# A linear-attention block with an MLP: two float32 products between the halves, done as hi and lo one-pass products

## The chip, the cores and the metric

The kernel runs on one core of a Trainium2 chip, in one launch. The metric is the device time in microseconds. Before the change three runs took 881.53, 881.9 and 882.74 us, so the median is 881.9 us. The engines that matter are TensorE (PE; its weight loads are shown as PEld), VectorE (DVE), ScalarE (ACT), GpSimd (POOL) and SyncE (SP), which issues all the DMAs here.

## What is computed

The input is one sequence of 2048 tokens of width 448. Two layers run, each a linear attention block (half A) and a GELU MLP (half B), both behind a layer norm and with a residual.

```python
def _A_ref(x, wqkv, wo):                       # H = 16 heads, Dh = 28
    qkv = (x @ wqkv) ...                       # q, k, v per head
    phi = lambda t: jnp.where(t > 0, t + 1, jnp.exp(t)) + 1e-6
    pq, pk = phi(q), phi(k)
    kv = jnp.einsum("bhsd,bhse->bhde", pk, v)
    z = jnp.einsum("bhsd->bhd", pk)            # sum of pk over the tokens
    num = jnp.einsum("bhqd,bhde->bhqe", pq, kv)
    den = jnp.einsum("bhqd,bhd->bhq", pq, z)[..., None] + 1e-6
    return (num / den) ... @ wo

x = x + _A_ref(_layernorm(x), A_wqkv, A_wo)
x = x + _B_ref(_layernorm(x), B_w1, B_b1, B_w2, B_b2)   # gelu(x @ w1 + b1) @ w2 + b2
x = x + _A_ref(_layernorm(x), A_wqkv, A_wo)
x = x + _B_ref(_layernorm(x), B_w1, B_b1, B_w2, B_b2)
```

## The kernel before

Tokens are worked in 16 tiles of 128. Nearly every matrix product is done with float32r operands, which TensorE takes in one pass. To keep the precision, an operand is split into a hi part (the value rounded to float32r, a copy) and a lo part (what is left, a subtraction), and a product is the sum of hi times hi, hi times lo and lo times hi, three one-pass products into the same PSUM bank. A few products are done in native float32 instead: the transposes, kvp, and the two that this change is about, zp and mp.

A layer has three parts. In **phase 1** (phase1, L542) each tile is normalised, k is projected (psk), phi is applied, the result pk is split into kh and kl, and the product G of x (xnh, xnl) with pk is accumulated in four PSUM banks over all tiles (stage_g, L473, four groups c = 0 to 3). VectorE also adds pk into za (L444). Most of the tiles' q projections (psq) are done here too and their phi is stored to DRAM as pq; the last seven are kept back to fill TensorE later. In the first layer the MLP's weights are split in the background (ScalarE copies w2h, GpSimd subtracts w2l, L352 and L353).

Then comes the **transition**, whose order is written out by hand in the string ORDER (L491). Each token calls one small function, and every engine runs its instructions in the order in which they are called:

- Q: a q projection of a kept-back tile. Qp (fill_qphi, L462): its phi, three ScalarE operations and one GpSimd addition (eq, L470), and the store to DRAM.
- G: the last tile's part of the product G.
- z (trans_z, L610): zp = ones times za, so that each of 128 partitions holds the sum of z over all tokens; ScalarE copies it to zb; VectorE makes dc from it.
- gt (L620): ScalarE copies the four banks of G to SBUF. kv (L627): kvp, the product of wv with gt, all heads at once. mask (L634): VectorE keeps the blocks on the diagonal of each head, in kvm.
- m0 to m3 (trans_m, L640): mp = kvm times wo, one group g of 112 rows each. ms (trans_ms, L645): its split into Mh (ScalarE) and Ml (VectorE).
- ld0 to ld3: loads of pq and x of the four tiles of block 0. qz (q_z, L681): GpSimd multiplies pq with zb, giving pz. qs (q_scale, L685): VectorE sums pz per head (dn, L689), adds dc (L690), takes the reciprocal (L692) and scales pq (L694). tq (L697): TensorE transposes the scaled pq into a PSUM bank. qq (q_split, L706): its split into qh (ScalarE) and ql (VectorE).
- o0 to o3 (o_mm, L716): pq times M, twelve one-pass products a tile. la, lb, T, x: residual, layer norm, transpose and split for the MLP.

zp, kvp and the tq share two PSUM banks (tag "m"), taken in turn, so a tq waits until the bank of the one before last has been read, which is when that tile's ql is done. mp and the output products share four (tag "acc").

The third part is the **MLP** (mlp1 L780, mlp2 L799): four blocks of four tiles, 14 steps each, with the next block's attention output worked behind it.

SBUF buffers are shared by tags: "E" and "F" (two each) hold kh and kl, "xn" (two) the background weights in the first layer and later the normalised rows, "H" (nine) the rows of x, "W6" kvm.

Of the kernel before, what the change touches and what calls it, by code (L numbers as in the profile page):

```python
# [10 lines left out]
F32R = mybir.dt.float32r  # L11
AF = mybir.ActivationFunctionType
OP = mybir.AluOpType
# [9 lines left out]
def linear_attn_mlp_kernel(  # L23
# [12 lines left out]
    pe, act, dve, pool, sp = nc.tensor, nc.scalar, nc.vector, nc.gpsimd, nc.sync  # L36
# [25 lines left out]
    def bank(tag, bufs, name):  # L62
        return psum.tile([128, 512], F32, name=name, tag=tag, bufs=bufs)
# [3 lines left out]
    def t448(tag, bufs, name, dt=F32):  # L67
        bufs = NH if tag == "H" else bufs
        return work.tile([128, D], dt, name=name, tag=tag, bufs=bufs)

    def t512(tag, bufs, name, dt=F32):
        return work.tile([128, 512], dt, name=name, tag=tag, bufs=bufs)

    def f(ap):
        return ap.bitcast(F32)
# [4 lines left out]
    def load_x(l, t):  # L80
        xt[l, t] = t448("H", 8, f"x{l}_{t}")
        sp.dma_start(xt[l, t], x_d[l][t * 128:(t + 1) * 128, :])
# [67 lines left out]

    ones = consts.tile([128, 128], F32, name="ones")
    dve.memset(ones, 1.0)
    warm = bank("m", 2, "warm")

    def warm_up(n):
# [295 lines left out]
    def stage_q(l, t, cs=range(4)):  # L451
        qs_[l, t] = proj("q", ("a", l, t // 4), t % 4, qs_.get((l, t)), cs)
        if 3 in cs:
            qo.append((l, t, qs_.pop((l, t))))

    def stage_qphi():
        while qo:
            l, t, o = qo.pop(0)
            e = phi(o, "eq")
            sp.dma_start(pq_d[l][t * 128:(t + 1) * 128, :], e)  # L460

    def fill_qphi():  # L462

        l, t, o = qo.pop(0)
        e = t512("e", 3, "eq")[:, :D]
        p = t512("E", 2, "ep")[:, :D]
        act.activation(e, o, AF.Relu, scale=-1.0)
        act.activation(p, o, AF.Relu)
        act.activation(e, e, AF.Exp, scale=-1.0)
        pool.tensor_tensor(e, p, e, op=OP.add)  # L470
        sp.dma_start(pq_d[l][t * 128:(t + 1) * 128, :], e)

    def stage_g(l, t, acc):  # L473
        h, lo = split.pop((l, t))
        kh, kl = ks.pop((l, t))
        first, last = t == 0, t == NT - 1
        for c in range(3):
            s = slice(c * 128, (c + 1) * 128)
            pe.matmul(acc[c], h[:, s], kh, start=first, stop=False)  # L479
            pe.matmul(acc[c], h[:, s], kl, start=False, stop=False)  # L480
            pe.matmul(acc[c], lo[:, s], kh, start=False, stop=last)  # L481
        pe.matmul(acc[3], h[:, TL:], kh, start=first, stop=False)
        pe.matmul(acc[3], h[:, TL:], kl, start=False, stop=last)

# [2 lines left out]


    ORDER = (  # L491
# [4 lines left out]
    )  # L496
# [110 lines left out]
            sp.dma_start(s, wo[h * 2 * G:(h + 1) * 2 * G, :].rearrange("(g p) n -> p g n", p=G))  # L607
            tr.wo += [s[:, 0], s[:, 1]]

    def trans_z(tr, za):  # L610
        zp = bank("m", 2, "zp")[:, :D]
        pe.matmul(zp, ones, za, start=True, stop=True)
        tr.zb = consts.tile([128, D], F32, name="zb", tag="za")
        act.activation(tr.zb, zp, AF.Identity, bias=zc)

        tr.dc = consts.tile([128, H], F32, name="dc", tag="dc")
        dve.tensor_reduce(tr.dc, tr.zb.rearrange("p (h d) -> p h d", d=DH), axis=mybir.AxisListType.X, op=OP.add)
        dve.tensor_scalar(tr.dc, tr.dc, 1e-6, 1e-6, op0=OP.mult, op1=OP.add)

    def trans_gt(tr, acc):  # L620
        tr.gt = []
        for c in range(4):
            s = t512("A" if c < 2 else "B", 2, "gt")[:, :D]
            act.copy(s, acc[c])
            tr.gt.append(s)
# [8 lines left out]
    def trans_mask(tr):  # L634
# [2 lines left out]
                          tr.kvp.rearrange("p (g d) -> p g d", g=NG),  # L637
                          mask[:, None, :].to_broadcast([G, NG, G]), op=OP.mult)

    def trans_m(tr, g):  # L640
        mp = bank("acc", 4, "mp")[:G, :D]
        pe.matmul(mp, tr.kvm[:, g * G:(g + 1) * G], tr.wo[g], start=True, stop=True)
        tr.mp[g] = mp

    def trans_ms(tr, g):  # L645
        if g == 0:
            tr.Mh, tr.Ml = [], []
        if g % 2 == 0:
            for n in ("Mh", "Ml"):
                s = work.tile([128, 1024], F32R, name=n, tag="S", bufs=5)  # L650
                getattr(tr, n).extend(s[:G, i * D:(i + 1) * D] for i in range(2))
        act.copy(tr.Mh[g], tr.mp[g])
        dve.tensor_sub(tr.Ml[g], tr.mp[g], f(tr.Mh[g]))

# [21 lines left out]
    def load_pq(l, b, j):  # L676
        t = b * 4 + j
        pqt[l, t] = t448(f"W{j}", 1, f"pq{l}_{t}")
        sp.dma_start(pqt[l, t], pq_d[l][t * 128:(t + 1) * 128, :])
# [36 lines left out]
    def o_mm(l, b, j, tr):  # L716
        qh, ql = qs.pop((l, b, j))
        o = ops[l, b, j] = bank("acc", 4, "op")[:, :D]
        for g in range(NG):
            s = slice(g * 128, (g + 1) * 128)  # L720
            pe.matmul(o, qh[:, s], tr.Mh[g], start=(g == 0), stop=False)
            pe.matmul(o, qh[:, s], tr.Ml[g], start=False, stop=False)
            pe.matmul(o, ql[:, s], tr.Mh[g], start=False, stop=(g == NG - 1))

    def oc_mm(l, b, j, tr):

# [175 lines left out]
    warm_up(2)  # L902

    for l in range(LAYERS):
        tr = SimpleNamespace(mp={})
        za, acc = phase1(l, tr)
        if l == 0:
            background(0)
        fill = list(range(DEFER, NT))

        def pre(j):
            for k in range(4):
                load_pq(l, 1, k)
            if l == 0:
                background(2)

        tok_ = SimpleNamespace(
            Q=lambda j: stage_q(l, fill.pop(0)), Qp=lambda j: fill_qphi(), Qv=lambda j: stage_qphi(), G=lambda j: stage_g(l, NT - 1, acc),
            ld=lambda j: (load_pq(l, 0, j), load_x(l, j)), z=lambda j: trans_z(tr, za), gt=lambda j: trans_gt(tr, acc),
            kv=lambda j: trans_kv(tr), mask=lambda j: trans_mask(tr), m=lambda j: trans_m(tr, j),  # L920
            ms=lambda j: trans_ms(tr, j), qz=lambda j: q_z(l, 0, j, tr), qs=lambda j: q_scale(l, 0, j, tr),
            tq=lambda j: q_transpose(l, 0, j), qq=lambda j: q_split(l, 0, j), o=lambda j: o_mm(l, 0, j, tr),
            la=lambda j: o_ln(l, 0, j), lb=lambda j: o_n(l, 0, j), T=lambda j: m_transpose(l, 0, j),
            x=lambda j: m_split(l, 0, j), pre=pre)
        for tok in ORDER.split():
            name, j = tok.rstrip("0123456789"), int("0" + tok.lstrip("abcdefghijklmnopqrstuvwxyzQTG"))
            getattr(tok_, name)(j)
        assert not fill and not qo
        table(AF.Gelu_apprx_tanh)
        q_z(l, 1, 0, tr)  # L930
        mlp1(l, 0, 0)
        trans_chunks(tr)
        for b in range(NB):
            acc = [bank("acc", 4, f"y{j}")[:, :D] for j in range(4)]
            nxt = b + 1 < NB
            if not nxt and l + 1 < LAYERS:
                st_k = stage_square(wqkv[:, D:2 * D])
                st_q = stage_square(wqkv[:, :D])
                load_to(l + 1, PRE - 1)
            for i in range(NF):  # L940
                if i + 1 < NF:
                    mlp1(l, b, i + 1)
                elif nxt:
                    mlp1(l, b + 1, 0)
                if l == 0 and b == 0 and i:
                    background(1, 1)
                if i == NF - 2 and not nxt and l + 1 < LAYERS:
                    table(AF.Exp)
                if 9 <= i < 13:
                    add_bias(l, b, i - 9)  # L950
                if nxt:
                    behind(l, b, i, tr)
                elif l + 1 < LAYERS:
                    if i == 2:
                        split_kq("k", st_k)
                    if i == 5:
                        split_kq("q", st_q)
                    if i in (3, 4, 6, 7, 8):
                        t = (3, 4, 6, 7, 8).index(i)
                        stage_a(l + 1, t)  # L960
                        stage_n(l + 1, t)
                        stage_t(l + 1, t)
                        if t % 2:
                            stage_sp(l + 1, t)
                    if 9 <= i < 13:
                        stage_x(l + 1, i - 9)
                mlp2(l, b, i, acc)
# [28 lines left out]
```

## Time and profile before

| | us |
|---|---|
| median of three runs | 881.9 |
| profiled execution, its own time | 881.78 |
| its span, from the first to the last instruction | 880.1 |
| TensorE busy in the span | 871.8 |
| transition, first layer (from zp to the MLP's first product) | 106.7 to 141.0 |
| transition, second layer | 538.5 to 572.8 |
| TensorE idle in each transition | 0.36 |

The profile is one execution. A busy share is the part of the span in which an engine had an instruction running. The timeline gives each instruction's start and length, in us from the span's start. The chain of waits follows what ended last back to the start. TensorE's one-pass products are pipelined: of 448 columns, one is shown with 0.37 us, but the next starts about 0.20 us after it, so their cost is read from start to start. A native float32 product is shown as two instructions (x2 for zp, x8 for the four mp). TensorE's granted clock was 1.00 in all of the transition.

In the transitions of the second layer VectorE was busy 24.8 of the 31.6 us from 538.5 to 570.1, ScalarE 13.8, and GpSimd 10.0.

### The profile page before, as it was taken

To read this page: it belongs to the slowest core of one execution; us is meant where nothing else is said; L and a number is where in the kernel's file an instruction comes from. 1 tells how busy PE (TensorE), PEld (TensorE's weight loads), DVE (VectorE), ACT (ScalarE), POOL (GpSimd) and SP (SyncE) were. 2 spreads that over 40 slices of the span, in tenths; PEclk is the share of its full clock that TensorE was granted. 3 is DMA by queue.
4 is the path that set the end of the run, shared out by engine and by line. 5 is a ranking of instruction groups with operands and counts; after the bars stand their busy time and mean duration, and the time that the engine had idled before them with its cause. 6 is when DMAs were issued, how large, how long until landed. Compare 5 with 4: busy or idle time off the path is not lost.

```text
span 880.1 us, 11693 instructions
## 1 busy us (share of the span) xinstructions
PE 871.8 (99%) x4190; PEld 773.4 (88%) x4190; DVE 485.6 (55%) x947; ACT 344.8 (39%) x609; POOL 221.1 (25%) x252
## 2 busy tenths in 40 slices
PE   8999999999999999999999999999999999999998
PEld 6999988888888888888899999888888888888887
DVE  6878585658455543226467866755574473432112
ACT  6576645324223322333355664442233133223221
POOL 5466633335012102011222333220220140140000
PEclk9999999999999999999999999999999999999999
DMA  5477715624413402051146443243332323111001
GB/s 156 148 213 223 218 53 159 199 78 140 132 59 104 156 0 96 1 178 48 48 136 196 153 144 95 63 152 101 104 114 91 112 75 131 49 49 40 3 1 42
DMA packets 62762, 93.71 MB, mean 106 GB/s; under 512 B 8816, under 2 KB 57968, under 8 KB 62704
## 3 DMA queue, kind: packets, MB, share of 16 engines
q1 hardware_dynamic: 62704, 92.97, 33.7%
q8 instruction: 33, 0.54, 0.3%
q14 instruction: 25, 0.20, 0.1%
HBM read 55.65 MB, written 34.08 MB: 102 GB/s over the span
## 4 chain that ended last, share of the span: by engine, by line
PE 96%; DVE 1%; POOL 1%; DMA 1%; ACT 1%; issue 0%; SPq 0%; POOLq 0%; ACTq 0%; DVEq 0%
PE y L806 10%; PE y L805 10%; PE y L804 10%; PE hp L787 9%; PE hp L786 9%; PE hp L788 9%; PE hp L789 3%; PE hp L790 3%; PE G L480 2%; PE G L481 2%; PE G L479 2%; PE psk L306 2%; PE psk L308 2%; PE psk L307 2%; PE psq L306 2%; PE psq L307 2%
## 5 line engine op out<-in xcount | busy, mean ns | idle before, releaser
L796 DVE TENSOR_TENSOR gl<-g,gh 128x512 fp32r<-128x512 f32 x112 | 82.7, 738 | 299.7 <-ACT gh L795 299.7
L792 ACT ACTIVATE g<-hp,b1s 128x512 f32<-128x512 f32 x112 | 77.0, 688 | 406.4 <-PE hp L790 406.4
L806 PE MATMUL y<-w2h,gl 128*128 128x448 f32 x448 | 163.9, 366 | 0.0
L805 PE MATMUL y<-w2l,gh 128*128 128x448 f32 x448 | 163.8, 366 | 0.0
L804 PE MATMUL y<-w2h,gh 128*128 128x448 f32 x448 | 163.8, 366 | 0.0
L787 PE MATMUL hp<-XH,w1l 128*128 128x512 f32 x336 | 131.7, 392 | 0.0
L786 PE MATMUL hp<-XH,w1h 128*128 128x512 f32 x336 | 131.4, 391 | 0.0
L788 PE MATMUL hp<-XL,w1h 128*128 128x512 f32 x336 | 131.2, 391 | 0.0
L203 POOL TENSOR_TENSOR brs<-bve,mhalf 128x1 f32<-128x1 f32 x64 | 38.9, 607 | 272.5 <-DVE bve L201 265.4
L804 PEld LDWEIGHTS y<-w2h,gh 128*128 128x128 f32 x448 | 84.2, 188 | 8.8
L805 PEld LDWEIGHTS y<-w2l,gh 128*128 128x128 f32 x448 | 84.3, 188 | 8.3
L806 PEld LDWEIGHTS y<-w2h,gl 128*128 128x128 f32 x448 | 84.3, 188 | 6.5
L788 PEld LDWEIGHTS hp<-XL,w1h 128*128 128x128 f32 x336 | 63.1, 188 | 13.6
L787 PEld LDWEIGHTS hp<-XH,w1l 128*128 128x128 f32 x336 | 63.2, 188 | 11.1
L786 PEld LDWEIGHTS hp<-XH,w1h 128*128 128x128 f32 x336 | 63.3, 188 | 10.9
L795 ACT CAST gh<-g 128x512 fp32r<-128x512 f32 x112 | 69.7, 622 | 3.6
L416 POOL TENSOR_TENSOR xnl<-x,xnh 128x384 fp32r<-128x384 f32 x32 | 35.7, 1117 | 84.4 <-ACT xnh L415 50.0
L683 POOL TENSOR_TENSOR pz<-pq,zb 128x448 f32<-128x448 f32 x32 | 36.6, 1148 | 79.7 <-DVE dn L689 65.3
L296 DVE TENSOR_TENSOR XL<-sp,XH 128x512 fp32r<-128x512 f32 x50 | 42.7, 861 | 5.3 <-ACT XH L295 5.3
L790 PE MATMUL hp<-XL,w1x 128*128 128x512 f32 x112 | 43.6, 389 | 0.0
L789 PE MATMUL hp<-XH,w1x 128*128 128x512 f32 x112 | 43.6, 389 | 0.0
L752 POOL TENSOR_TENSOR x<-x,b2b 128x448 f32<-128x448 f32 x32 | 41.9, 1332 | 0.0
(145 smaller groups left out, 1565.6 us busy)
## 6 DMA issues: line engine op xcount, KB each, us to landing
x<-in_A_x_dram SPq DMA_DIRECT2D x32, 224.0 KB, 3.7
pq_d<-eq SPq DMA_DIRECT2D x32, 224.0 KB, 2.9
pq<-pq_d SPq DMA_DIRECT2D x32, 224.0 KB, 3.2
x<-x_d SPq DMA_DIRECT2D x32, 224.0 KB, 3.6
sq_a<-sq SPq DMA_DIRECT2D x13, 512.0 KB, 2.9
sp<-sq_a SPq DMA_DIRECT2D x52, 128.0 KB, 3.0
sq_q<-sq SPq DMA_DIRECT2D x12, 512.0 KB, 2.6
sp<-sq_q SPq DMA_DIRECT2D x48, 128.0 KB, 3.1
```

The lines of the kernel that those rows point to most:

```text
L296: dve.tensor_sub(lo.rearrange("p (c i n) -> p c i n", c=4, n=32), x, f(h))
L786: pe.matmul(o, w1h[:, c, s], x.moving(x.hi, c), start=(c == 0), stop=False)
L787: pe.matmul(o, w1l[:, c, s], x.moving(x.hi, c), start=False, stop=False)
L788: pe.matmul(o, w1h[:, c, s], x.moving(x.lo, c), start=False, stop=False)
L789: pe.matmul(o, w1x[:, s], x.moving(x.hi, 3), start=False, stop=False)
L790: pe.matmul(o, w1x[:, s], x.moving(x.lo, 3), start=False, stop=True)
L792: act.activation(g, hp, AF.Gelu_apprx_tanh, bias=b1s[:, i:i + 1])
L795: act.copy(gh, g)
L796: dve.tensor_sub(gl, g, f(gh))
L804: pe.matmul(acc[j], gh[:, s], w2h[:, i], start=first, stop=False)
L805: pe.matmul(acc[j], gh[:, s], w2l[:, i], start=False, stop=False)
L806: pe.matmul(acc[j], gl[:, s], w2h[:, i], start=False, stop=last)
```

## The change

zp becomes two one-pass products, of ones with zh and with zl, the hi and lo parts of za; the ones get a float32r copy. mp becomes three for each group: kvh with woh, kvh with wol, kvl with woh. The splits are new work: zh, the four woh and kvh are copies on ScalarE, zl and kvl subtractions on VectorE, and the four wol subtractions on GpSimd. They take buffers from the tags E, F, xn and H. In ORDER the new tokens zs, kvs, wh and wl place them; the last tile's G is divided, its group c = 0 stands ahead of z and the others behind it; and the groups of m, ms and o_mm go in the order 2, 3, 0, 1.

```diff
+    ones_r = consts.tile([128, 128], F32R, name="ones_r")
+    dve.tensor_copy(ones_r, ones)
...
-    def stage_g(l, t, acc):
+    def stage_g(l, t, acc, cs=range(4)):
...
     ORDER = (
-        "Q ld1 z ld0 ld2 qz0 qz1 G gt qs1 Q Qp kv qs0 tq1 Q mask qz2 tq0 qs2 ld3 "
-        "m0 qq1 Qp m1 qz3 ms0 qq0 m2 ms1 m3 ms2 tq2 ms3 qs3 o0 la0 qq2 o1 tq3 lb0 la1 qq3 Qp pre "
+        "Q ld1 zs G0 z ld0 ld2 qz0 qz1 G1 wh2 wh3 gt qs1 wl2 wl3 Q Qp kv qs0 tq1 wh0 wh1 Q mask kvs qz2 wl0 wl1 tq0 qs2 ld3 "
+        "m2 qq1 Qp m3 qz3 ms2 qq0 m0 ms3 m1 ms0 tq2 ms1 qs3 o0 la0 qq2 o1 tq3 lb0 la1 qq3 Qp pre "
...
-    def trans_z(tr, za):
+    def trans_zs(tr, za):
+        tr.zh = t512("F", 2, "zh", F32R)[:, :D]
+        tr.zl = t512("E", 2, "zl", F32R)[:, :D]
+        act.copy(tr.zh, za)
+        dve.tensor_sub(tr.zl, za, f(tr.zh))
+
+    def trans_z(tr):
         zp = bank("m", 2, "zp")[:, :D]
-        pe.matmul(zp, ones, za, start=True, stop=True)
+        pe.matmul(zp, ones_r, tr.zh, start=True, stop=False)
+        pe.matmul(zp, ones_r, tr.zl, start=False, stop=True)
...
+    def trans_kvs(tr):
+        tr.kvh = t512("E", 2, "kvh", F32R)[:G, :D]
+        tr.kvl = t448("H", 8, "kvl", F32R)[:G]
+        act.copy(tr.kvh, tr.kvm)
+        dve.tensor_sub(tr.kvl, tr.kvm, f(tr.kvh))
+
+    def trans_wh(tr, g):
+        tr.woh[g] = t512("F" if g < 2 else "xn", 2, "woh", F32R)[:G, :D]
+        act.copy(tr.woh[g], tr.wo[g])
+
+    def trans_wl(tr, g):
+        tr.wol[g] = t448("H", 8, "wol", F32R)[:G]
+        pool.tensor_tensor(tr.wol[g], tr.wo[g], f(tr.woh[g]), op=OP.subtract)
+
     def trans_m(tr, g):
         mp = bank("acc", 4, "mp")[:G, :D]
-        pe.matmul(mp, tr.kvm[:, g * G:(g + 1) * G], tr.wo[g], start=True, stop=True)
+        s = slice(g * G, (g + 1) * G)
+        pe.matmul(mp, tr.kvh[:, s], tr.woh[g], start=True, stop=False)
+        pe.matmul(mp, tr.kvh[:, s], tr.wol[g], start=False, stop=False)
+        pe.matmul(mp, tr.kvl[:, s], tr.woh[g], start=False, stop=True)
...
-        for g in range(NG):
+        for g in (2, 3, 0, 1):
```

More of the change, by code (lines that the diff above doesn't have):

```diff
@@ L471, in fill_qphi @@
         sp.dma_start(pq_d[l][t * 128:(t + 1) * 128, :], e)
-    def stage_g(l, t, acc):
-        h, lo = split.pop((l, t))
-        kh, kl = ks.pop((l, t))
+    def stage_g(l, t, acc, cs=range(4)):
+        h, lo = split[l, t]
+        kh, kl = ks[l, t]
         first, last = t == 0, t == NT - 1
-        for c in range(3):
+        for c in cs:
+            if c == 3:
+                pe.matmul(acc[3], h[:, TL:], kh, start=first, stop=False)
+                pe.matmul(acc[3], h[:, TL:], kl, start=False, stop=last)
+                continue
             s = slice(c * 128, (c + 1) * 128)
@@ L481, in stage_g @@
             pe.matmul(acc[c], lo[:, s], kh, start=False, stop=last)
-        pe.matmul(acc[3], h[:, TL:], kh, start=first, stop=False)
-        pe.matmul(acc[3], h[:, TL:], kl, start=False, stop=last)
     ORDER = (
[2 rows of a table removed]
[2 rows of a table added]
         "o2 T0 lb1 la2 o3 x0 T1 Q lb2 la3 x1 T2 Q x2 lb3 Qp "
@@ L638, in trans_mask @@
                           mask[:, None, :].to_broadcast([G, NG, G]), op=OP.mult)
+    def trans_kvs(tr):
[9 more added lines that the diff above has]
+        pool.tensor_tensor(tr.wol[g], tr.wo[g], f(tr.woh[g]), op=OP.subtract)
     def trans_m(tr, g):
         mp = bank("acc", 4, "mp")[:G, :D]
-        pe.matmul(mp, tr.kvm[:, g * G:(g + 1) * G], tr.wo[g], start=True, stop=True)
+        s = slice(g * G, (g + 1) * G)
+        pe.matmul(mp, tr.kvh[:, s], tr.woh[g], start=True, stop=False)
+        pe.matmul(mp, tr.kvh[:, s], tr.wol[g], start=False, stop=False)
+        pe.matmul(mp, tr.kvl[:, s], tr.woh[g], start=False, stop=True)
         tr.mp[g] = mp
     def trans_ms(tr, g):
-        if g == 0:
-            tr.Mh, tr.Ml = [], []
         if g % 2 == 0:
-            for n in ("Mh", "Ml"):
-                s = work.tile([128, 1024], F32R, name=n, tag="S", bufs=5)
-                getattr(tr, n).extend(s[:G, i * D:(i + 1) * D] for i in range(2))
+            for m in (tr.Mh, tr.Ml):
+                s = work.tile([128, 1024], F32R, name="M", tag="S", bufs=5)
+                m[g], m[g + 1] = (s[:G, i * D:(i + 1) * D] for i in range(2))
         act.copy(tr.Mh[g], tr.mp[g])
@@ L718, in o_mm @@
         o = ops[l, b, j] = bank("acc", 4, "op")[:, :D]
-        for g in range(NG):
+        for g in (2, 3, 0, 1):
             s = slice(g * 128, (g + 1) * 128)
-            pe.matmul(o, qh[:, s], tr.Mh[g], start=(g == 0), stop=False)
+            pe.matmul(o, qh[:, s], tr.Mh[g], start=(g == 2), stop=False)
             pe.matmul(o, qh[:, s], tr.Ml[g], start=False, stop=False)
-            pe.matmul(o, ql[:, s], tr.Mh[g], start=False, stop=(g == NG - 1))
+            pe.matmul(o, ql[:, s], tr.Mh[g], start=False, stop=(g == 1))
     def oc_mm(l, b, j, tr):
@@ L904, in linear_attn_mlp_kernel @@
     for l in range(LAYERS):
-        tr = SimpleNamespace(mp={})
+        tr = SimpleNamespace(mp={}, Mh={}, Ml={}, woh={}, wol={})
         za, acc = phase1(l, tr)
@@ L917, in linear_attn_mlp_kernel @@
         tok_ = SimpleNamespace(
-            Q=lambda j: stage_q(l, fill.pop(0)), Qp=lambda j: fill_qphi(), Qv=lambda j: stage_qphi(), G=lambda j: stage_g(l, NT - 1, acc),
-            ld=lambda j: (load_pq(l, 0, j), load_x(l, j)), z=lambda j: trans_z(tr, za), gt=lambda j: trans_gt(tr, acc),
+            Q=lambda j: stage_q(l, fill.pop(0)), Qp=lambda j: fill_qphi(), Qv=lambda j: stage_qphi(),
+            G=lambda j: stage_g(l, NT - 1, acc, range(1, 4) if j else (0,)), zs=lambda j: trans_zs(tr, za),
+            kvs=lambda j: trans_kvs(tr), wh=lambda j: trans_wh(tr, j), wl=lambda j: trans_wl(tr, j),
+            ld=lambda j: (load_pq(l, 0, j), load_x(l, j)), z=lambda j: trans_z(tr), gt=lambda j: trans_gt(tr, acc),
             kv=lambda j: trans_kv(tr), mask=lambda j: trans_mask(tr), m=lambda j: trans_m(tr, j),
```

## The prediction

> **What bounds the kernel now.** I read the page first: its busy shares and the shares of the chain that ended last.
>
> ```profile
> PE 871.8 (99%) x4190; PEld 773.4 (88%) x4190; DVE 485.6 (55%) x947; ACT 344.8 (39%) x609; POOL 221.1 (25%) x252
> PE 96%; DVE 1%; POOL 1%; DMA 1%; ACT 1%; issue 0%; SPq 0%; POOLq 0%; ACTq 0%; DVEq 0%
> ```
>
> TensorE sets the time. Whatever shortens its own work is gained whole, and every wait put into its queue is lost whole. So I read the chain of waits in order of time (start us, us, what), here the middle part of the second layer.
>
> ```profile
> 538.67 0.75 PE zp L612 x2
> 543.87 3.14 PE kvp L632 x32
> 547.01 0.44 PE tq L701 x4
> 550.12 3.01 PE mp L642 x8
> 553.13 0.44 PE tq L701 x4
> ...
> 570.46 0.47 PE psq L306
> ```
>
> The two products that the change touches cost 0.75 us (zp) and 3.01 us (four mp), and from 538.5 to 570.1 TensorE never stands. The other engines have slack there, but how much depends on whether two of them can work at once. The timeline of VectorE (start, us, what), early in the MLP:
>
> ```profile
> 148.89 0.17 DVE L690 TENSOR_TENSOR dn<-dn,dc 128x16 f32<-128x16 f32 x1
> 149.38 1.18 DVE L694 SCALAR_TENSOR_TENSOR pq<-pq,rd 128x448 f32<-128x448 f32 x1
> ...
> 153.78 0.48 DVE L690 TENSOR_TENSOR dn<-dn,dc 128x16 f32<-128x16 f32 x1
> 154.58 1.23 DVE L694 SCALAR_TENSOR_TENSOR pq<-pq,rd 128x448 f32<-128x448 f32 x1
> ```
>
> and of GpSimd in the same stretch:
>
> ```profile
> 148.93 1.15 POOL L683 TENSOR_TENSOR pz<-pq,zb 128x448 f32<-128x448 f32 x1 [5.67 <-DMA wq<-Ml]
> 153.03 1.19 POOL L353 TENSOR_TENSOR w2l<-stg,w2h 128x448 fp32r<-128x448 f32 x1 [2.95 <-DMA wq<-Mh]
> 154.19 1.15 POOL L683 TENSOR_TENSOR pz<-pq,zb 128x448 f32<-128x448 f32 x1
> ```
>
> The same L690 takes 0.17 or 0.48 us and L694 0.62 (below) or 1.18 and 1.23. The long ones start inside a GpSimd instruction and end just after it: pz ends at 150.08, L694 at 150.56. A VectorE operation with both operands in SBUF waits for a running GpSimd operation; it gets in between two of them (L690 of 153.78 ends at 154.26, between w2l and pz). A blocked 0.62 us operation ends 0.48 us after the GpSimd one. Operations that read PSUM (kl L440, Ml L653) keep 0.62 us whatever GpSimd does. The Trainium skill, page "SBUF — State Buffer", section "Who interferes with whom", states this as an exclusive lock: two SBUF inputs on VectorE against a GpSimd instruction that reads SBUF, the first to start holds it for its whole length. By that rule the sum is the 886.5 us below, without it the 880.0 us of the first rival; the rows above agree with it.
>
> **What it removes on TensorE.** One-pass products of 448 columns start every 0.2035 us (eleven of psq: 536.28 to 538.51). zp: two of them, 0.41 for 0.75, gain 0.34. mp: 12 x 0.2035 = 2.44 for 3.01, gain 0.57. Together 0.91 a layer, 1.8 us in two. The Trainium skill, "TensorE: Matmul & The Clock Gate", section "Back-to-back issue gap", gives N/2.4 + 2.5 ns, an estimate of 0.189 us; by it the 14 products would save 0.2 us more a layer and the sum would be 886.1; the rows decide for 0.2035.
>
> **What it adds.** Per layer on ScalarE six copies (zh, four woh, kvh), SBUF to SBUF, 0.56 us each and 0.46 to the next (w2h L352, xnh L415); on VectorE zl and kvl, both operands in SBUF, 448 wide: between 0.62 (L694) and 0.67 (XL L296, 512 wide), taken 0.62; on GpSimd four wol, 1.13 to 1.20 by w2l L353, taken 1.15 with 1.11 to the next. The one copy into ones_r lies ahead of the warm-up where VectorE then waits 2.4 us for the first x; at most 0.3 us if that cover were gone. No DMA is added. On SP's queue the store of the first eq waits for GpSimd and the loads of pq3 and x3 stand behind it: eq ends 0.7 us later (below), pq3 lands near 546.4 + 3.2 = 549.6, and its use is at 552.1. The G group put ahead of zp and the new order of the mp groups (2, 3, 0, 1) move TensorE's work without adding any. woh 2 and 3 stand ahead of the four gt on ScalarE: these then end at 540.35 + 2 x 0.46 + 4 x 0.44 = 543.0 and kvp starts at 543.4, so 0.4 us of cover; were it gone, kvp would wait by what is over. woh's buffers are free by then (the last background w2l ends at 107.72, woh starts after 108.4).
>
> **The path, second layer** (times of this trace, shifted by hand). za is ready at 537.92, zh to 538.51, zl to 539.16 with GpSimd idle; TensorE does its first G group meanwhile and needs zl at 539.32. No wait. The last zp product starts 539.32, so zb ends 540.35 instead of 540.09. GpSimd: pz 540.43 and 541.55, wol 542.66 and 543.77 to 544.92. VectorE: dn ends 543.35, L690 is blocked to 543.85, L694 to 545.40. eq, held by L694, ends 546.41 (a held GpSimd operation gets in 0.12 before the recorded end: xnl at 94.35). The next L690 ends 546.45; pz runs to 547.50 and blocks L694 to 547.98. Then wol 0 to 549.01, wol 1 from 548.97 to 550.12. kvm follows L694, to 548.51, kvh on ScalarE to 549.10, and **kvl is ready at 549.13, 0.16 us after wol 1 started**: blocked to 550.60. TensorE, 0.33 us earlier than before, starts the first mp at 549.63 and needs kvl at 550.04. With 0.1 for the weight load that is no longer ahead (psq of 570.46 takes 0.47 for 0.37): a wait of **0.7 us**.
>
> What is late next is the scaling of the third tile. Before, it slipped in ahead of GpSimd:
>
> ```profile
> 548.85 0.62 DVE L694 SCALAR_TENSOR_TENSOR pq<-pq,rd 128x448 f32<-128x448 f32 x1
> 549.39 0.68 DVE L711 TENSOR_TENSOR ql<-tq,qh 112x512 fp32r<-112x512 f32 x1
> 551.48 0.62 DVE L653 TENSOR_TENSOR Ml<-mp,Mh 112x448 fp32r<-112x448 f32 x1 [1.40 <-ACT Mh L652]
> ```
>
> ```profile
> 549.50 1.13 POOL L470 TENSOR_TENSOR eq<-ep,eq 128x448 f32<-128x448 f32 x1 [2.72 <-ACT eq L469]
> 550.58 1.14 POOL L683 TENSOR_TENSOR pz<-pq,zb 128x448 f32<-128x448 f32 x1
> ```
>
> Now dn follows kvl, to 551.13. The second eq comes at 551.05 (its three ScalarE steps stand behind kvh and qh) and runs to 552.18: L690 to 552.22, reciprocal to 552.50; pz runs 552.14 to 553.27: L694 to 553.75; then ql to 554.36. The transpose tq of the third tile uses the PSUM bank that ql frees. TensorE would be there at 552.77 and gets it at 554.4, with the weight load 554.5: **1.7 us**. Behind it the first output product needs ql of the other tile, which stands behind ql and the first Ml: 555.55 against 555.34, with the weight load 0.3; the next Ml 0.1. The wait at psq (570.46) may grow by 0.1. Sum 2.9, less 0.91: **+2.0 us**.
>
> **First layer.** The same chain, and one wait more: zl is ready at 106.76 while the second w2l runs (105.48 and 2.24 us for two, to 107.72). It ends at 108.20; TensorE needs it at 107.54: 0.7 us. So **+2.7**. Both layers +4.7: the span 880.1 becomes 884.8, and with the 1.7 us around it (881.78 less 880.1) **886.5 us**. The profiled execution stands 0.1 under the median of 881.9.
>
> **Rivals.**
> 1. *Faster.* The added subtractions run beside each other. Place: kvl, the L694 scalings and zl; if VectorE's two-SBUF operations weren't held, every step above would end ahead of TensorE's need, and only the saving is left: 881.8 - 1.8 = 880.0. Unheld, kvp's end at 546.7 would give kvl by 546.7 + 0.61 + 0.56 + 0.62 and hand-overs, 548.6, against 550.04: it decides where the holds up to kvl add less than 1.4 us, and those before the third tq as little. For it: 55% and 25% busy shares. Against: L694's median is 1.18 us over 32 instructions.
> 2. *kvl gets in before wol 1.* The margin is 0.16 us in a chain of a dozen hand-overs. Then kvl ends at 549.75 and costs nothing, wol 1 ends near 550.8, and L694 of the third tile is ready at 551.13, just when eq (551.05) is. Behind eq it gives tq at 553.4 against 552.07, ahead of it 552.45: a wait of 1.3 or 0.4 where the forecast has 2.4. Per layer 1.1 to 2.0 less: 884.3 to 882.5.
> 3. *Worse.* VectorE loses twice running in one place of the path, or the late Ml and ql hold the output products longer: one GpSimd operation, 1.1 us, more per layer: 888.7. Against: L690 at 153.78 got its turn.
> 4. *A tie.* Half the holds fall away (stalls of 1.0 a layer against 0.91): 881.9 or so.
>
> **How the numbers follow.** Forecast 0.62, its own range 885.2 to 888. Rival 2: 0.17; rival 3: 0.08; rival 1: 0.08; rival 4: 0.05. A difference below 0.2% (1.8 us) can't be told from none. Slower 0.62 + 0.17 + 0.08 = 0.87, same 0.05, faster 0.08. The range reaches from rival 2's lower end, 882.6, to rival 3, 888.9, and leaves out rivals 1 and 4, 0.13, and something for misjudged sizes.
>
> **What would show it.** Right: zp two products 0.2 us apart, mp twelve; the first mp's third product waiting on kvl in both layers; tq of the third tile waiting on VectorE for over 1 us; zl long (over 1 us) in the first layer alone; kvl about 1.5 us beside a wol. Wrong: kvl at 0.62 beside a running wol kills the lock and with it the sum (rival 1). If kvl comes before the last wol, it is rival 2. If waits stand elsewhere (gt, kvp, the first transposes), the path is wrong though the size might be right.

## The result and the profile after

The changed kernel takes 889.1 us (median of 6 runs, 887.79 to 891.82) where the kernel before took 881.7 in the same session: a ratio of 1.0084, 95% interval 1.0073 to 1.0096. The sign was forecast; the time was forecast at 886.5, with a range from 882.6 to 888.9 that the measured time lies just above.

The profiled execution of the changed kernel is its fastest run, 887.79 us, with a span of 886.1. From the page, the busy shares and the shares of the chain that ended last:

```profile
PE 872.7 (98%) x4198; PEld 772.5 (87%) x4198; DVE 495.6 (56%) x952; ACT 350.8 (40%) x621; POOL 230.7 (26%) x260
PE 81%; DVE 6%; issue 4%; DMA 4%; POOL 3%; ACT 1%; SPq 1%; POOLq 0%; DVEq 0%; ACTq 0%
```

Before, TensorE held 96% of that chain. Now 15 points have gone to other engines: somewhere TensorE stands and others set the end. (The chain is followed back from the last instruction and runs over the other engines for a long way once it has left TensorE, so the 15 points are not lost time.) What TensorE waited for (line, releaser: us in total, times, longest) names the places:

```profile
PE tq L727 <- DVE ql L737: 3.0, 2, 1.5
PE mp L670 <- DVE kvl L655: 1.6, 2, 0.8
PE zp L623 <- DVE zl L618: 0.6, 1, 0.6
```

These are three of the waits that were forecast, in the forecast places, two of them in both layers. The timeline of TensorE in the second layer (start us, us, engine, line, out<-in, at the end the idle time ahead and its releaser) shows the products and what they wait for:

```profile
542.24 0.37 PE L622 MATMUL zp<-zh,ones_r 128*128 128x448 f32 x1
542.44 0.45 PE L623 MATMUL zp<-zl,ones_r 128*128 128x448 f32 x1
...
553.18 0.46 PE L668 MATMUL mp<-woh,kvh 112*112 112x448 f32 x1
553.48 0.37 PE L669 MATMUL mp<-wol,kvh 112*112 112x448 f32 x1
554.65 0.46 PE L670 MATMUL mp<-woh,kvl 112*112 112x448 f32 x1 [0.80 <-DVE kvl L655]
554.95 0.37 PE L668 MATMUL mp<-woh,kvh 112*112 112x448 f32 x1
555.15 0.36 PE L669 MATMUL mp<-wol,kvh 112*112 112x448 f32 x1
555.35 0.36 PE L670 MATMUL mp<-woh,kvl 112*112 112x448 f32 x1
```

From start to start the two products of zp and, behind the wait, those of mp cost 0.20 us each, so the saving is there. The third product of the first group stands 0.80 us until kvl is done. VectorE's timeline of the same stretch says why kvl is late:

```profile
546.60 0.45 DVE L716 TENSOR_TENSOR dn<-dn,dc 128x16 f32<-128x16 f32 x1
547.09 0.25 DVE L718 RECIPROCAL rd<-dn 128x16 f32<-128x16 f32 x1
547.38 2.32 DVE L720 SCALAR_TENSOR_TENSOR pq<-pq,rd 128x448 f32<-128x448 f32 x1
...
550.76 1.23 DVE L720 SCALAR_TENSOR_TENSOR pq<-pq,rd 128x448 f32<-128x448 f32 x1
551.92 0.61 DVE L647 TENSOR_TENSOR kvm<-kvp,mask 112x448 f32<-112x448 f32 x1
553.16 1.43 DVE L655 TENSOR_TENSOR kvl<-kvm,kvh 112x448 fp32r<-112x448 f32 x1 [0.63 <-ACT kvh L654]
```

and GpSimd's beside it:

```profile
545.87 2.26 POOL L663 TENSOR_TENSOR wol<-wot,woh 112x448 fp32r<-112x448 f32 x2
548.07 1.15 POOL L472 TENSOR_TENSOR eq<-ep,eq 128x448 f32<-128x448 f32 x1
550.36 1.15 POOL L709 TENSOR_TENSOR pz<-pq,zb 128x448 f32<-128x448 f32 x1 [1.14 <-issue]
551.47 2.64 POOL L663 TENSOR_TENSOR wol<-wot,woh 112x448 fp32r<-112x448 f32 x2
```

kvl starts at 553.16 inside the last wol (to 554.11) and ends at 554.59, 0.48 us behind it: the hold that was forecast, 1.43 us for an operation of 0.62. Above it is a line that was not forecast. The first tile's scaling L720 starts at 547.38 inside the second wol, which ends at 548.13. It does not get in when that ends. GpSimd's eq runs first, to 549.22, and the scaling ends 0.48 us behind that one: 2.32 us, where the prediction has it end 0.48 us behind the wol, after some 1.25. The first layer has the same, 2.33.

To see what each part costs, the span is cut at four points: the start of the q projection just ahead of zp and the first product of the MLP, in each layer. The two stretches between such points are the transitions. The stretch from the first MLP to the second transition is 395.25 us in both traces and the last one, from the MLP of layer 1 to the end, 307.3, so the difference lies in the rest:

| us | before | after | difference |
|---|---|---|---|
| launch and phase 1, layer 0 | 104.5 | 103.9 | -0.6 |
| transition, layer 0 | 36.5 | 40.2 | +3.7 |
| transition, layer 1 | 36.5 | 39.4 | +2.9 |
| span | 880.1 | 886.1 | +6.0 |

The forecast had +2.7 and +2.0. Each layer lost 0.9 to 1.0 us more than that. And the median lies 1.3 above this profiled run, which the table can't explain. Both were put to the test.

### The profile page after: what moved, and what is told of

It is laid out like the page before. It is cut to its first block, busy times and chain, and to the rows that moved or that the text cites. A ratio compares the mean times of both kernels' runs of the same rounds, so it can differ in the third digit from the quotient of the medians.

```text
span 886.1 us, 11737 instructions
## 1 busy us (share of the span) xinstructions
PE 872.7 (98%) x4198; PEld 772.5 (87%) x4198; DVE 495.6 (56%) x952; ACT 350.8 (40%) x621; POOL 230.7 (26%) x260
## 4 chain that ended last, share of the span: by engine, by line
PE 81%; DVE 6%; issue 4%; DMA 4%; POOL 3%; ACT 1%; SPq 1%; POOLq 0%; DVEq 0%; ACTq 0%
PE y L832 10%; PE y L831 10%; PE y L830 10%; PE hp L813 9%; PE hp L812 9%; PE hp L814 9%; PE hp L816 3%; PE hp L815 3%; PE op L759 2%; PE op L758 2%; PE op L760 2%; PE psq L308 1%; PE psq L310 1%; PE psq L309 1%; PE psk L309 1%
## 5 line engine op out<-in xcount | busy, mean ns | idle before, releaser
L709 POOL TENSOR_TENSOR pz<-pq,zb 128x448 f32<-128x448 f32 x32 | 36.8, 1151 | 83.1 <-DVE dn L715 70.7
```

## The experiments

All were timed beside the kernel before, on one chip in each session, and they are compared by ratios within a session. The median of the kernel before was 881.45 us in the first session (four kernels), 881.9 in the second (four) and 881.78 in the third (two).

**Without the wol subtractions.** The second product of each group uses woh in place of wol, so TensorE has the same work, but the kernel leaves out the lo part of wo and can serve for timing alone.

```diff
-        tr.wol[g] = t448("H", 8, "wol", F32R)[:G]
-        pool.tensor_tensor(tr.wol[g], tr.wo[g], f(tr.woh[g]), op=OP.subtract)
+        tr.wol[g] = tr.woh[g]
```

> Leaves out the four wol subtractions on GpSimd in each layer; the second of the three mp products uses woh in place of wol, so TensorE's work is the same. Theory (GpSimd's subtractions hold VectorE's two-SBUF operations): L720 of the first tile falls from 2.32 us to under 1.3, kvl from 1.43 to about 0.62, the waits of mp on kvl (0.8 a layer) and of tq on ql (1.5 a layer) go, only the wait on zl in the first layer (0.6) stays: saving 1.8, cost 0.6, so about 880.6 us. Rival (the other added work is late by itself: two subtractions on VectorE, six copies on ScalarE): the waits of mp and tq stay for the greater part, over 885 us.

Measured: 880.53 us, ratio 0.9991 (0.9981 to 1.0000). VectorE's timeline in the second layer:

```profile
543.78 0.62 DVE L719 SCALAR_TENSOR_TENSOR pq<-pq,rd 128x448 f32<-128x448 f32 x1
...
548.22 0.63 DVE L655 TENSOR_TENSOR kvl<-kvm,kvh 112x448 fp32r<-112x448 f32 x1 [0.63 <-ACT kvh L654]
```

The same two operations take 0.62 and 0.63 us, with TensorE's waits on kvl and ql gone. The transition of layer 1 is 35.6 us, 0.9 under that of before: the 0.91 of the saving, whole. Layer 0 keeps its wait on zl (0.6 us) and gains 0.1 (36.4 us). So the loss hangs on the four GpSimd subtractions a layer, and the one-pass products are a gain in the trace; the time itself, whose interval reaches 1.0000, can hardly be told from no change.

**wol on 128 partitions.** Extra rows of wo are loaded and subtracted too; no product uses them.

```diff
+            sp.dma_start(s[G:], wo[h * 32:(h + 1) * 32, :].rearrange("(g p) n -> p g n", p=16))
...
-        tr.wol[g] = t448("H", 8, "wol", F32R)[:G]
+        tr.wol[g] = t448("H", 8, "wol", F32R)
```

> The four wol subtractions are done on 128 partitions in place of 112 (the rows above 112 get other rows of wo and are not used), all else as in the changed kernel. Of all cases in the two traces where a VectorE operation waits behind a GpSimd one that another follows at once, the first L720 (2.32 us, behind wol and then eq) is the only one in which VectorE didn't get in between. Theory: the 112-partition wol lets the following 128-partition eq in first; then L720 falls to about 1.2 us and the time by 0.9 us a layer, to about 887.2. Rival: eq itself, or the turn, decides it: L720 stays at 2.3 us and the time at 889.

Measured: 887.26 us, ratio 1.0074 (1.0047 to 1.0101); the profiled run 886.12 with a span of 884.4. VectorE, then GpSimd:

```profile
546.31 1.22 DVE L722 SCALAR_TENSOR_TENSOR pq<-pq,rd 128x448 f32<-128x448 f32 x1
```

```profile
544.80 2.25 POOL L664 TENSOR_TENSOR wol<-wot,woh 128x448 fp32r<-128x448 f32 x2
547.00 1.52 POOL L472 TENSOR_TENSOR eq<-ep,eq 128x448 f32<-128x448 f32 x1
```

Now VectorE has its turn behind the second wol and it is eq that is held (1.52 us for 1.15). It isn't that the scaling came at another moment: it starts 0.75 us ahead of the end of the wol with 112 rows and 0.74 with 128. The scaling is back at 1.22 in both layers. TensorE's wait on kvl halves to 0.4, and the other 0.4 us are gained just ahead of it, in short stalls at the second tile's transpose and the first mp. The transitions are 39.4 and 38.6 us, +2.9 and +2.1 on before, where the prediction had +2.7 and +2.0. All that was altered is the number of rows of one operation, of the copy ahead of it, and two loads. So 0.8 of the 0.9 to 1.0 us a layer came from whose turn it was behind the second wol, and 0.1 to 0.2 is left for prices misjudged elsewhere.

**TensorE kept busy in its waits.** Unused products of the kind that follows, three ahead of zp in layer 0, four ahead of the first mp group and eight ahead of the last.

```diff
+        for _ in range({2: 4, 1: 8}.get(g, 0)):
+            pe.matmul(mp, tr.kvh[:, s], tr.woh[g], start=True, stop=True)
```

> TensorE gets products that nobody uses where it waits in the changed kernel: 3 ahead of zp in the first layer (0.6 us), 4 ahead of the first mp group (0.8 us) and 8 ahead of the last one (1.6 us) in each layer. Theory (the six timed runs of the changed kernel lie from 887.8 to 891.8 because the granted clock falls for a time after the waits in some of them): the clock is 0.999 in every run and all lie within 1 us of 888. Rival (the spread has nothing to do with the waits): spread and clocks as in the changed kernel, and the added 5.4 us of products that don't fit the waits show as up to 1 us more.

Measured: 888.82 us (887.86 to 889.09), ratio 1.0082 (1.0067 to 1.0097). No wait on zl, kvl or ql is left in the list, and the transitions stay as they were, 40.2 and 39.4: VectorE sets their length, not TensorE. The mean granted clock was 0.999 to 1.000 in all four runs, which lie within 1.3 us of each other, two of them just outside the 1 us around 888 that the theory allows. The median moved too little to say that the clock had a share. In this profile phase 1 of layer 1 took 1.6 us longer than in that of the changed kernel, at a full clock (the last point of this text), and that alone puts its 889.07 us above 887.8.

**The changed kernel again**, in the same session.

> The changed kernel as it is, beside the others on one chip. Both theories: about 1.0084 times the kernel before, 887.8 to 891.8 us in single runs, granted clocks of 0.996 to 0.999, with the lower clock in the longer runs if the clock makes the spread.

Measured: 889.54 us, ratio 1.0097 (1.0079 to 1.0115). This time the profile caught one of the long executions, 891.56. Busy time by stretches (PE, PEld, DVE, ACT, POOL, then the granted TensorE clock, the DMA share and GB/s):

```profile
123.00:125.00 2.00, 0.50 (x3) 0.13 (x2) 2.00 (x3) 0.94 (x3) 0.73 (x1) 1.00 0.30 115
126.00:129.00 3.00, 3.00 (x10) 2.70 (x9) 2.90 (x7) 0.00 (x0) 0.00 (x0) 0.50 0.02 5
130.00:134.00 4.00, 4.00 (x23) 3.68 (x22) 3.76 (x9) 1.48 (x5) 0.55 (x1) 1.00 0.00 0
...
562.80:566.00 3.20, 3.20 (x10) 2.85 (x9) 2.58 (x7) 0.59 (x1) 0.00 (x0) 0.50 0.00 0
```

Behind the wait of 1.5 us for ql (to 124.87) the clock is granted at half, for 3.41 us (125.72 to 129.13), and the same comes in layer 1. TensorE gets through 10 products in 3 us where it does 17 once the clock is back. The transitions are 41.3 and 40.9 us against 40.2 and 39.4, so this costs 1.1 and 1.4 us. The remaining 1.2 us of this long execution lie ahead of the first transition (105.1 us for 103.9), where the clock is full. In the other profile of the same kernel the same waits leave the clock at 1.00. Half a clock for 3.41 us takes 0.002 off the mean over 890 us, so a mean of 0.998 stands for one such stretch and 0.996 for two. Over the ten runs of the changed kernel the two with a mean granted clock of 0.999 took 887.8 and 888.2 us, the eight with 0.996 to 0.998 took 889.0 to 891.8.

**The sum of z alone.** The product with wo is native again, in the old place.

```diff
-        pe.matmul(mp, tr.kvh[:, s], tr.woh[g], start=True, stop=False)
-        pe.matmul(mp, tr.kvh[:, s], tr.wol[g], start=False, stop=False)
-        pe.matmul(mp, tr.kvl[:, s], tr.woh[g], start=False, stop=True)
+        pe.matmul(mp, tr.kvm[:, g * G:(g + 1) * G], tr.wo[g], start=True, stop=True)
```

> The sum of z in hi and lo alone; the product with wo is one native product again, and no wo is split. Theory (each part's effect by itself, all of the loss in the wo part): each layer's zp saves 0.34 us, the wait for zl in the first layer gives back 0.6, so the span is about 0.1 us below before's and the time within 0.2% of 881.5 (881.0 to 882.2); VectorE's first-tile scaling takes 1.2 us or less, and the granted clock holds 1.0 through both transitions. Rival (the z part carries a part of the loss, by its conversions on ScalarE and its two one-pass products): 883 or more.

Measured: 881.61 us, ratio 1.0001 (0.9992 to 1.0010), as the theory said. The transitions are 36.9 (+0.4) and 36.2 (-0.3): the second layer gains the 0.34 and the first gives more than that to the wait for zl.

**The product with wo alone.**

```diff
-        pe.matmul(zp, ones_r, tr.zh, start=True, stop=False)
-        pe.matmul(zp, ones_r, tr.zl, start=False, stop=True)
+        pe.matmul(zp, ones, za, start=True, stop=True)
```

> The product with wo in hi and lo alone; the sum of z is one native product again. Theory: all waits on kvl (0.8 us in each layer) and on the third tile's turn (1.5 each) stay, the first-tile scaling takes 2.3 us in both layers, and 0.68 us of the saving goes while the wait of 0.6 for zl goes too, so the stretch from the Q to the first hp is about 3.3 us longer than before's in each layer: span about 886.5, median 888 to 890, with the clock halved for some 3.4 us behind the waits in most executions. With the run of the z part alone the two differences from before add up to that of the changed kernel within 1 us. Rival (the parts need each other, the zl subtraction and its place shift the order of VectorE's turns): under 886.5.

Measured: 889.23 us, ratio 1.0082 (1.0068 to 1.0096). The first tile's scaling takes 2.26 and 2.27 us, the waits on kvl and ql are 0.8 and 1.5 in each layer, and this profile has the halved clock in layer 1 (41.0 us there, 39.7 in layer 0). The four times don't follow the clock, though, and only two show the halved clock that most were expected to have: 888.93 us at 0.997, 888.96 at 1.000, 889.49 at 0.998, 889.58 at 0.999. The differences of the two parts, -0.3 and +7.3, add up to 7.0, against 7.4 and 8.1 for the whole change in its two sessions. The loss is all in the second part; the last 0.4 to 1.1 us lie within what the runs of one kernel scatter.

**wol on 128 partitions and the waits filled**, both edits together, with two and seven unused products ahead of the mp groups.

> The wo rests made on 128 partitions, as in the earlier run, and unused products in TensorE's waits: three ahead of zp in the first layer, two ahead of the first mp group, seven ahead of the last. Theory (what is left of the loss above the waits is TensorE's clock at half for 3.4 us after a wait): every execution has a mean granted clock of 0.999 or more, the times lie together from 885.8 to 887.5, median about 886.4. Rival (the clock has no share in the median): the executions scatter as those without the fill did (886.1 to 891.1), or the median is 887.3 or more.

Measured: 886.48 us (886.32 to 887.53), ratio 1.0054 (1.0041 to 1.0066), clock 0.999 or more in all five runs. Without the fill the same kernel scattered from 886.1 to 891.1 us, at clocks of 1.000 to 0.996 in the order of the times. In the two kernels with unused products all nine runs have 0.999 or more; in the three like them without (the changed kernel, wol on 128 partitions, the product with wo alone) six of eighteen have. So the unused products, which shorten nothing, keep the clock up, and in this kernel the long executions are gone. The transitions (39.4 and 38.6) are as without the fill. With the turn and the clock put right the kernel stands at the 886.5 of the prediction; that it does so to 0.1 us is luck, since runs of one kernel scatter by more than 1 us.

**wol made ahead, in phase 1 of layer 0**, stored to DRAM and read back in each transition. The background work of phase 1 is spread over the steps anew to take them in.

```diff
+                hi = t512("e", 3, "wh", F32R)[:G, :D]
+                act.copy(hi, s)
+                pool.tensor_tensor(s.bitcast(F32R), s, f(hi), op=OP.subtract)
+                sp.dma_start(wol_d[g], s)
...
-        pool.tensor_tensor(tr.wol[g], tr.wo[g], f(tr.woh[g]), op=OP.subtract)
+        sp.dma_start(f(tr.wol[g]), wol_d[g])
```

> The wo rests are made once, by four subtractions on GpSimd early in phase 1 of layer 0 (beside the w1 splits), written to DRAM and read back in each transition, so that no long GpSimd subtraction stands in the transition. Theory (the GpSimd subtractions there are the whole loss): as the run without them, 880.5 (880.0 to 881.5); no wait on kvl or ql on TensorE, the wait of 0.6 for zl stays in the first layer. Rival (the four reads of 0.2 MB in the transition come late, or the four subtractions and loads in phase 1 push its chain): TensorE waits on wol, or the stretch to the first Q grows, 882.5 or more.

Measured: 888.53 us, ratio 1.0071 (1.0057 to 1.0085): the rival. The transitions are good, 36.8 and 35.6 us, but launch and phase 1 take 111.8 us instead of 103.9. What TensorE waited for there, ScalarE's instruction ahead of the first of these waits, and the stretches around it:

```profile
PE psk L309 <- ACT XH L298: 1.5, 1, 1.5
PE G L497 <- DVE kl L453: 1.0, 2, 0.8
PE psk L311 <- DVE XL L299: 0.5, 1, 0.5
```

```profile
65.55 0.62 ACT L298 CAST XH<-sp 128x512 fp32r<-128x512 f32 x1 [2.12 <-DMA sp<-sq_a]
```

```profile
62.00:66.00 4.00, 2.71 (x14) 2.17 (x12) 0.62 (x1) 1.84 (x4) 1.16 (x1) 1.00 0.98 260
...
68.00:71.00 3.00, 3.00 (x8) 2.17 (x8) 2.70 (x6) 2.56 (x6) 1.86 (x4) 0.50 0.27 103
```

The loads and stores come where the DMA engines are 98% busy, the read-back of the next rows (sp) is late, and behind TensorE's wait the clock is halved here too. The waits (3.0 us) and half of the 3.4 us at half clock make 4.7 of the 7.9 us; the rest was not traced.

**Layer 1 alone, wol made in the MLP of layer 0.** The same four subtractions beside the last w2 splits; layer 0 keeps its native products.

```diff
+        if l == 0:
+            pe.matmul(mp, tr.kvm[:, s], tr.wo[g], start=True, stop=True)
+            return
```

> Layer 0 as before the change (native products); layer 1 with both products in hi and lo, its wo rests made on GpSimd during the first MLP block of layer 0, written to DRAM and read back in the transition. Theory (the GpSimd subtractions beside VectorE's chain are the whole loss, the one-pass products a real gain of 0.91 us a layer): no wait on kvl, ql or zl in layer 1; its stretch from the Q to the first hp is 0.9 us shorter than before's, the span 0.9 less, the time about 881.0 where before is 881.9. Rival (reading the rests back, or the four subtractions in the MLP block, costs as much as the products save): same as before or more, 881.9 to 884.

Measured: 880.90 us, ratio 0.9990 (0.9980 to 1.0001). The transition of layer 1 is 35.6 us, 0.9 under before's, no wait on zl, kvl or ql. The trace has what the theory said; the time by itself can't be told from no change. The run also shows a turn behind one of its subtractions of 112 rows, with an operation of 128 rows next (GpSimd, then VectorE):

```profile
216.48 1.52 POOL L365 TENSOR_TENSOR stg<-stg,wh 112x448 fp32r<-112x448 f32 x1 [1.85 <-issue]
217.96 1.15 POOL L801 TENSOR_TENSOR x<-x,b2b 128x448 f32<-128x448 f32 x1
```

```profile
217.54 0.49 DVE L738 TENSOR_TENSOR dn<-dn,dc 128x16 f32<-128x16 f32 x1
```

Here VectorE's short addition, of 16 columns, did get in (it ends at 218.03, 0.03 us behind the subtraction). So 112 rows followed by 128 don't by themselves give GpSimd the turn.

**The same, and the sum of z in hi and lo in both layers**, with the two w2 subtractions moved behind the second pz of layer 0.

```diff
-        "Q ld1 z ld0 ld2 qz0 qz1 G0 G1 gt ..."
+        "Q ld1 zs G0 z ld0 ld2 qz0 qz1 bg G1 gt ..."
```

> As the run beside it, and the sum of z of layer 0 too in hi and lo, with the two w2 subtractions of GpSimd that stand beside zl moved behind the second pz. Theory: no wait for zl in either layer (its subtraction takes 0.6 us, not 1.4), another 0.34 us less, about 880.7. Rival (the two subtractions then block the first tiles' scalings, 1.2 us in place of 0.6 each, and VectorE's chain of layer 0 is late by as much): 881.2 to 882.5.

Measured: 880.81 us, ratio 0.9985 (0.9975 to 0.9996): the only one below before with its whole interval, by 1.0 us in the medians; an interval that clears 1 by 0.0004, in one run of ten, can be chance. The time is where the theory had it (880.7), but the trace isn't: zl takes 0.62 us and nobody waits for it, but the scalings of the first three tiles of layer 0 then take 1.28, 1.23 and 1.22 us (0.63, 1.22 and 0.63 before), and that transition is 36.7 us where 36.2 was hoped for. So the second move gained nothing over the run before it; the rival was right about the place.

## Why the prediction came out as it did

**The sign and the mechanism were right.** The two-SBUF operations of VectorE and the GpSimd subtractions do exclude each other, and without the subtractions the change gains 0.9 us in layer 1 and, with the wait on zl, 0.1 in layer 0. The forecast waits came. Counted as the prediction does, from start to start with the weight load, they are zl 0.8 (0.7 forecast, first layer only), kvl 1.0 (0.7) in both layers, the third tile's tq 1.7 (1.7). The turn has its share in kvl: with 128 rows it is 0.6. The saving of 0.91 a layer is what layer 1 shows in the run without wol. (Eleven psq products in 2.23 us are 0.2027 us each and not 0.2035, which changes 0.01 us a layer.) The Trainium skill's exclusive lock ("SBUF — State Buffer", "Who interferes with whom") agrees with the holds: 1.43 (kvl) and 1.41 us (zl) against 0.62 to 0.63. It doesn't account for the 2.33 us of the scaling, which was there before eq started.

**The step that failed: "it gets in between two of them".** The working gave VectorE the turn whenever a GpSimd operation ended, and with it L694 (now L720) at 1.23 us and "eq, held by L694". On the chip eq went first, in both layers, which cost 0.8 us a layer by the run with 128 rows, 1.6 us in all. It is the mechanism of rival 3, "VectorE loses twice running in one place of the path", which had 0.08. The row that argued against it was a turn of VectorE's short addition behind a 128-row subtraction (w2l at 153.03); the wol ahead of eq has 112 rows, and with 128 rows the scaling got its turn. In all eight transitions traced with 112 rows and the eq behind them the scaling took 2.26 to 2.33 us, in all four with 128 rows 1.22. Which rule of the chip lies behind that was not found, and it isn't the number of rows alone: in the same transitions the short addition (546.60, 0.45 us) gets in behind the first wol, with another of 112 rows next, and in layer 0 of the run with layer 1 alone one gets in between 112 and 128 rows.

**What the sum left out: the clock.** Every product was priced at a full clock, since it was 1.00 in all of the transition before. By their mean clocks, eight of the ten executions of the changed kernel had one such stretch of 3.41 us at half clock or two, at 1.1 to 1.4 us each. The prediction listed the waits ahead of it and did not ask what they do to the clock. That the 1.3 us between the profiled run and the median are the clock's is likely but not shown: no run of the changed kernel near its median was traced, with the waits filled the median is still 888.8, with the product with wo alone the times don't follow the clock, and the slower phase 1 can add as much.

Together: 886.5 + 1.6 (the turn) + 0.3 (the rest of the two transitions) - 0.6 (launch and phase 1, which differ by as much between executions) + 1.3 (profiled run to median) = 889.1. Each transition's own +2.7 and +2.0 measured +2.9 and +2.1 once the turn was put right.

## What to carry to other kernels

Work put on an idle GpSimd isn't free when VectorE has operations with both inputs in SBUF on the path: price each as one hold of VectorE, and, where a second GpSimd operation follows at once, as two at the upper bound. Moving the work ahead of the critical stretch, to a stretch with slack on DMA too, turned layer 1's loss of 2.9 us into a gain of 0.9; in a stretch with full DMA queues it cost more than it saved. A wait on TensorE costs its length and may cost the clock as well, so a forecast for this kernel that adds waits of 1.5 us should carry 1.1 to 1.4 us more for each of them as its upper end.

## What the hardware showed that was not expected

- Ahead of eq, the turn between two back-to-back GpSimd operations went to GpSimd behind a 112-row subtraction (scaling 2.3 us) and to VectorE behind a 128-row one (1.22). In the other turns shown here VectorE got in.
- TensorE's clock was halved behind a wait of 1.5 us, in some executions and not in others of the same kernel. In all four halved stretches traced that wait lies in the 3.41 us ahead of the stretch, and in the run with wol made ahead no other stands near it; the wait of 0.8 us on kvl, where there is one, lies earlier, and whether it has a part isn't shown. A wait of 1.4 to 1.5 us near 22 us halved the clock in none of the twelve profiles. The Trainium skill ("TensorE: Matmul & The Clock Gate", "What's actually happening") has the clock follow the activity in windows of about 3.4 us that run freely. The length of the slow stretch and its coming and going agree with that. Its section "Why this matters for your kernels" asks only for gaps under about 3 us; here one of 1.5 us was enough at times.
- In some executions the products of most of a phase 1 come slightly slower at a granted clock of 1.00. The same 60 us of phase 1 of layer 1, in the trace before and in that of the run with layer 1 alone:

```profile
460.00:520.00 60.00, 60.00 (x298) 55.71 (x297) 46.12 (x100) 35.22 (x64) 17.44 (x28) 1.00 0.59 180
```

```profile
460.00:520.00 60.00, 60.00 (x292) 54.50 (x291) 45.23 (x98) 34.15 (x62) 17.27 (x27) 1.00 0.58 179
```

  292 products instead of 298 in the same time; the stretch from the MLP to the transition is 396.8 us instead of 395.25. It came in four of the twelve profiles (the changed kernel again in layer 0; in layer 1 the changed kernel with its waits filled, the run with layer 1 alone and the last one), none of them that of the kernel before, and its cause stays open. It is why one profile can stand 1.5 us off another with no difference in the transitions.
